# Left-over queries kept plain and scored on 64 rows per head, in an attention and maxout-FFN kernel

## The chip, the cores and the metric

The kernel runs on one core of one Trainium2 chip. The metric is the device time of one execution in microseconds. Before the change it is 326.37 us, the median of 8 runs (324.82 to 329.38).

## The reference, cut to what matters

Attention with a relative bias runs over 8 batches, 8 heads, 576 positions and 64 dimensions per head; its output, as 4608 tokens of 512, goes through a feed-forward layer with the maximum of three products.

```
scores = (q @ k.T) / 8 + bias[bucket(|i - j|)]     # per batch and head, 576 x 576
attn   = softmax(scores)                            # over the 576 keys
x      = attn @ v                                   # (8, 8, 576, 64) -> (4608, 512)
out    = max(x @ w1, x @ w2, x @ w3) @ w_out        # 512 -> 768 -> 512
```

## The kernel before

**Tiles.** 576 positions are four tiles of 128 and a rest of 64. The four tiles of keys and queries are the main part; the last 64 keys are the left-over keys, the last 64 queries the left-over queries. Two heads go together as a head pair: their 2 x 64 dimensions fill 128 partitions. For each batch b (0 to 7) and head pair hp (0 to 3) the loop of line 768 makes:

- two visits (`visit`, line 524): visit 0 scores queries 0 to 255, visit 1 queries 256 to 511, against the four key tiles. Each product runs on 64 rows, one head on partitions 0 to 63 and the other on 64 to 127, in pairs of matmuls that write different PSUM banks. ScalarE takes the exponential of each 128 x 1024 tile (`sc`).
- the left-over keys (`left_keys`, line 540): both heads at once on 128 rows. `ktail` holds the 64 keys of one head in one diagonal block and those of the other in the second, with zeros elsewhere (`diag`, line 145). They are scored for 640 query columns (512 and 128), into `el`, columns 0 to 639. The query side is kept in diagonal blocks as well (`qtail`), so the 64 left-over queries take 128 columns.
- the left-over queries (`left_queries`, line 556): four matmuls on 128 rows, each with 128 columns (64 of each head, zeros opposite), into a tile of the pool `ps_s`; one exponential writes `el` from column 640 on.
- the multiplications by exp(bias) near the diagonal, on VectorE (`times_band`, `times_bandt`, `times_band_left`).
- the products with v (`attend`, line 572), in two halves of queries, in banks of the pool `ps_a` (two buffers). A column of ones in v gives the sums; reciprocal and product (`quotients`) write `x_sb`. The half with queries 256 to 575 has two products with the left-over keys for the left-over queries (lines 594 to 598), one for each head, 65 columns each.

**Order.** The order of each engine's work is mostly written out (`inorder`). The products with v lag one head pair behind (`late`): half 0 of pair hp-1 comes after visit 0 of pair hp, half 1 after visit 1. Between visits `fill` puts groups of the FFN: each group is a `first`, `second` or `third` product of four 512-column matmuls (`ps0`, `ps1`, `ps2`), or an output block of six (`pso`), spread over the head pairs of the next batch. `fill` takes hooks, small functions that it calls before one of its groups: the last hook goes just before the last group, an earlier one before the group ahead of that. In the loop of line 768 the left-over keys are the hook of the fill after visit 0; the products with the bias for key tile 2, then the left-over queries, are the two hooks of the fill after visit 1.

**Loads.** GpSimd issues the loads of q, k and v and casts them to bf16 on the way: `load_qk` (line 162) and `load_v` (line 180). Left-over parts are loads of their own, one per parity of head (lines 160 and 170). For batches 2 to 7, SyncE then issues DMA transposes of q and k (`transposes`, line 438, issued at line 447), five steps of a q and a k transpose: steps 0 to 3 the main tiles, step 4 the left-over part of 128 rows. They are called during the batch before. In the same queue stand the transposes of the attention result (`xT<-x_sb`, line 619), issued after the quotients of the last head pair, that is in head pair 0 of the next batch, and the stores of the output (line 379). `load_v(b+1)` is called in head pair 2, 1 or 0 of batches 1, 2 and later, after visit 1 and before the fill; its target was last read by batch b-1's products with v. Batches 0 and 1 transpose on TensorE instead.

Of the kernel before, what the change touches and what calls it, by code (L numbers as in the profile page):

```python
# [39 lines left out]
def kernel(  # L40
# [12 lines left out]
    nc = tc.nc  # L53
# [64 lines left out]
    def constants(i):  # L118
        inorder(nc.vector.memset(ktail[i][:], 0.0))
        if i == 0:  # L120
            inorder(nc.vector.memset(qtail[i][:], 0.0))
        inorder(nc.vector.memset(vt[i][:], 0.0))
        inorder(nc.vector.memset(vx[i][:, :, :, D:AW], 1.0))
        for par in range(2):
            inorder(nc.vector.memset(vt[i][64 * par : 64 * par + 64, :, par, D:AW], 1.0))
# [22 lines left out]

    def q_diag(b, par, h0, h1):
        return diag(qtail[b % 2], par, h0, h1)  # L150

# [10 lines left out]
    def load_qk(b, behind=None):  # L162

        loads = []
        for t in range(KT):
            for src, dst in zip((q, k), batch[b]):
                loads.append(in_turn(b, nc.gpsimd.dma_start(out=dst[:, t], in_=main_part(src, b)[:, t])))  # L167
        for src, dst in ((q, q_diag), (k, k_diag)):
            for par in range(2):
                load = nc.gpsimd.dma_start(out=dst(b, par, 0, H), in_=tail_part(src, b, 0, H, par))  # L170
                loads.append(in_turn(b, load))
        if behind:
            for load in loads:
                tc.add_manual_dep(
                    load.ins, behind.ins.name,
                    mybir.DependencyInfo(mybir.DependencyClass.Sync, mybir.DependencyReason.DATA),
                    reason="these loads go behind the result's transposes",
                )
# [64 lines left out]
    constants(0)  # L243
    inorder(nc.vector.memset(qtail[1][:], 0.0))
    dve_copy(pick[:], ids[:])
# [15 lines left out]
    load_main(q, 0, 0, H, batch[0][0], 2, KT)  # L261
    load_tail(q, 0, 0, H, q_diag)
    load_v(0, 0, H)
# [38 lines left out]

    bandt = const.tile([P, HP, 2 * P], BF16, name="bandt")

    def make_bandt():
        for par in range(2):
            r = slice(64 * par, 64 * par + 64)
            c = BAND // 2 - 64 * par
            for c0, c1 in ((192, 256), (0, 192)):
                dve_copy(bandt[r, :, c0:c1], hank[r, par::2, c : c + c1 - c0][:, :, ::-1])  # L310

# [126 lines left out]
    def transposes(b):  # L438

        made = qk_tiles()  # L440
        qk.append(made)

        def one(j, t):
            src = batch[b][j][:, t].rearrange("p h d -> p (h d)") if t < KT else (
                (qtail, ktail)[j][b % 2][:].rearrange("p h c -> p (h c)")
            )
            inorder(nc.sync.dma_start_transpose(out=made[j][:, :, P * t : P * t + P], in_=src))

        for t in range(KT + 1):
            one(0, t)  # L450
            one(1, t)
            yield

    def qk_tiles():
        return [qkt.tile([P, HP, (KT + 1) * P], BF16, tag=n, name=n) for n in ("qT", "kT")]

# [24 lines left out]
    def more_transposes(hp):  # L481

        hs = slice(2 * hp, 2 * hp + 2)
        tp = ps_f.tile([P, 2 * CH], BF16, tag="ff", name="tp2")
        for t in range(2):
            tr(tp[:, P * t : P * t + P], batch[0][0][:, 2 + t, hs, :].rearrange("p h d -> p (h d)"), ident[:])
        tr(tp[:, QS : QS + P], qtail[0][:, hp, :], ident[:])
        dve_copy(qk[0][0][:, hp, QS:], tp[:, 0 : QS + P])

    def second_transposes(made, hp):  # L490
# [3 lines left out]
        for j, tl in enumerate((qtail, ktail)):  # L494
# [10 lines left out]
        tail = [  # L505
            copy(made[j][:, hp, KT * P :], tp[:, j, KT * P : (KT + 1) * P])
            for j, copy in enumerate((dve_copy, act_copy))
        ]
# [14 lines left out]

    def visit(qT, kT, e4, c, mid=None):


        for tt in range(0, KT, 2):
            sc = ps_s.tile([P, 2, 2, QS], F32, tag="sc", name="sc")
# [22 lines left out]
    def times_bandt(hp, el):  # L551
        inorder(nc.vector.tensor_tensor(
            out=el[:, S - 192 : S + 64], in0=el[:, S - 192 : S + 64], in1=bandt[:, hp, :], op=ALU.mult
        ))

    def left_queries(hp, qT, kT, el):

        sc = ps_s.tile([P, KT, 2 * 64], F32, tag="sc", name="scq")
        for t in range(KT):
            mm(sc[:, t, :], lhsT=kT[:, P * t : P * t + P], rhs=qT[:, QM : QM + P])  # L560
        eq = el[:, S + 64 :].rearrange("p (t h q) -> p t h q", t=KT, h=2)
        exp(eq, sc[:].rearrange("p t (h q) -> p t h q", h=2))

    def times_band_left(hp, el):
        last_tile = el[:, S + P * KT - 64 :].rearrange("p (h q) -> p h q", h=2)
        inorder(nc.vector.tensor_tensor(
# [5 lines left out]
    def attend(b, hp, e4, el, half):  # L572
# [19 lines left out]
        n = 2 + half  # L592
        if half:
            for par in range(2):
                mm(
                    x[:, 4 + par, :], lhsT=el[:, S - P + 64 * par :][:, 0:P], rhs=vl[:, hp, par, 0:AW],
                    start=True, stop=False, skip_group_check=True,
                )
                for kt in range(KT):
                    mm(  # L600
                        x[:, 4 + par, :], lhsT=el[:, S + P * kt + 64 * par :][:, 0:P],
                        rhs=v[:, kt, 2 * hp + par, 0:AW],
# [38 lines left out]
    def e_tiles():  # L641
        return (
            ep.tile([P, KT, 2, QM], BF16, tag="e4", name="e4"),
            ep.tile([P, S + 64 + KT * P], BF16, tag="el", name="el"),
        )
# [19 lines left out]
    def load_second():  # L665
        for h0, h1 in ((0, 2), (2, H)):
            load_packed(k, h0, h1, k_1)
            load_packed(q, h0, h1, q_1)
            if h0 == 0:
                load_tail(q, 1, 0, H, q_diag)  # L670
                load_tail(k, 1, 0, H, k_diag)
# [47 lines left out]
    for hp in range(HP):  # L719
# [14 lines left out]
        def keys():  # L734
            left_keys(hp, qT, kT, el, QS, S + 64)

# [31 lines left out]
    for b, hp in [(b, hp) for b in range(1, B) for hp in range(HP)]:  # L768
        if hp == 0:
            x_sb[b] = x_tile()  # L770
        qT, kT = (x[:, hp, :] for x in qk[b])
        e4, el = e_tiles()
        rate = 8 if b == 1 or (b, hp) == (2, 0) else 13

# [18 lines left out]
        if b == 1 and hp + 1 < HP:  # L793
            spread_packed(hp + 1, nc.vector)
        fill(rate, lambda: left_keys(hp, qT, kT, el, 0, S + 64))
        times_bandt(hp, el)


        visit(qT, kT, e4, 1)
        store_outputs()  # L800
# [3 lines left out]
        if turned:  # L804
            turned.pop(0)()
        quotients = next_late()
        times_band(hp, e4, 1, 0, QM, inorder)
        quotients()
        if b == 1 and hp + 1 < HP:
            second_transposes(qk[1], hp + 1)  # L810
        if hp == 1:
            add_ffn((b - 1) * CH if b > 1 else QS, CH if b > 1 else QS)
        if hp == (2, 1, 0)[min(b, 3) - 1] and b + 1 < B:
            load_v(b + 1, 0, H)
# [3 lines left out]
        if hp == 2 and 1 < b < B - 2:  # L818
            batch[b + 2] = load_tiles()
            load_qk(b + 2)  # L820

        def queries():
            left_queries(hp, qT, kT, el)
            times_band(hp, e4, 3, 0, QM, inorder)

        fill(rate, lambda: times_band(hp, e4, 2, 0, QM, inorder), queries)
        times_band_left(hp, el)
# [46 lines left out]
```

The softmax here doesn't subtract the row's maximum and nothing guards it: scores larger than these inputs give would overflow.

## Time and profile before

| what | value |
|---|---|
| time before, median of 8 runs | 326.37 us (324.82 to 329.38) |
| the profiled execution: its time, its span | 329.38 us, 327.6 us |
| TensorE matmul busy | 311.5 us, 95% of the span |
| VectorE, ScalarE, GpSimd busy | 66%, 62%, 34% |
| mean granted TensorE clock | 0.979 |
| start of visit 0, head pair 0, of batches 3 to 7 | 97.97, 133.88, 167.76, 201.64, 235.53 us |

Times within the trace count from the start of the span. A matmul row gives its latency; matmuls overlap in the pipe, so the distance between the starts of consecutive groups tells what a group occupies. The release of an engine by another is inferred from semaphore events. A DMA row of the queue SP or POOL shows the issue; the landing is later and is given apart.

### The profile page before, as it was taken

How to read it: one execution, taken by the hardware profiler on the slowest of the kernel's cores; microseconds unless marked ns; L12 is line 12 of the kernel's file. 1: busy time of each engine (PE TensorE's matmuls, PEld its weight loads, DVE VectorE, ACT ScalarE, POOL GpSimd, SP SyncE). 2: the span in 40 equal slices, each digit the busy share in tenths (PEclk: the TensorE clock that was granted, in tenths of full speed). 3: DMA queues.
4: the chain of work that ended last, by engine and by line, in shares of the span. 5: the costliest groups of instructions: out<-in, count | busy, mean ns of one | idle time of the engine just before them, and what ended most of it. 6: DMA issues, size and time to landing. Idle time of an engine off the chain costs nothing.

```text
span 327.6 us, 8019 instructions
## 1 busy us (share of the span) xinstructions
PE 311.5 (95%) x3232; PEld 177.1 (54%) x3232; DVE 216.5 (66%) x537; ACT 202.2 (62%) x274; POOL 113.0 (34%) x151
## 2 busy tenths in 40 slices
PE   7847999999997999999999999999999999999995
PEld 2335776787554555555555555555555554444442
DVE  6466788778665766776667777676667675554452
ACT  4837798788676667776776677757776661121221
POOL 8931967209756772096107810500000000000000
PEclk9869899999999999999999999999999999999999
DMA  9999999979999999999999999995132103301103
GB/s 166 171 207 198 152 156 132 147 141 118 159 166 155 161 159 191 133 109 168 209 96 102 180 208 78 97 186 145 13 66 83 55 3 67 136 0 64 66 0 128
DMA packets 165541, 40.72 MB, mean 124 GB/s; under 512 B 155384, under 2 KB 161024, under 8 KB 165504
## 3 DMA queue, kind: packets, MB, share of 16 engines
q0 software_dynamic: 103904, 16.66, 77.0%
q1 hardware_dynamic: 59840, 23.08, 38.1%
q10 hardware_dynamic: 1760, 0.47, 0.7%
q8 instruction: 25, 0.41, 0.5%
q14 instruction: 12, 0.10, 0.1%
HBM read 35.39 MB, written 9.45 MB: 137 GB/s over the span
## 4 chain that ended last, share of the span: by engine, by line
PE 82%; DMA 6%; ACT 3%; POOL 3%; DVE 3%; issue 1%; SPq 0%; POOLq 0%; ACTq 0%
PE ps L94 40%; PE a L94 15%; PE pso L94 13%; PE sc L94 9%; DMA kT<-k_sb 3%; PE sct L94 3%; DMA vt<-in_v_dram 2%; ACT e L522 2%; PE scq L94 2%; POOL q_sb L143 1%; POOL vx L143 1%; DVE e L516 1%; PE tp L97 1%; DMA out_dram<-osb 1%; ACT el L522 1%
## 5 line engine op out<-in xcount | busy, mean ns | idle before, releaser
L94 PE MATMUL ps<-xT,w_bf 128*128 128x512 bf16 (+1 forms) x720 | 156.6, 359 | 0.0
L522 ACT ACTIVATE e<-sc 128x1024 bf16<-128x1024 f32 x128 | 124.5, 1025 | 26.7 <-PE sc L94 26.1
L94 PEld LDWEIGHTS <-w_bf 128*128 128x128 bf16 x720 | 66.1, 98 | 57.1 <-issue 1.5
L516 DVE TENSOR_TENSOR e<-e,hank 128x512 bf16<-128x512 bf16 (+2 forms) x136 | 59.7, 467 | 27.3 <-ACT e L522 24.8
L337 ACT ACTIVATE m<-ps 128x512 bf16<-128x512 f32 x54 | 32.3, 599 | 66.8 <-PE ps L94 64.5
L343 DVE TENSOR_TENSOR m<-ps,m 128x512 bf16<-128x512 f32 x54 | 37.3, 691 | 45.9 <-ACT el L522 24.5
L94 PEld LDWEIGHTS <-kT 64*128 64x128 bf16 (+1 forms) x704 | 35.8, 96 | 41.2 <-issue 23.7
L94 PE MATMUL pso<-wo_bf,hT 128*128 128x512 bf16 (+2 forms) x222 | 51.0, 373 | 0.0
L94 PE MATMUL a<-vx,e 128*128 128x65 bf16 x1024 | 46.0, 195 | 0.0
L94 PE MATMUL sc<-qT,kT 64*128 64x256 bf16 x512 | 41.6, 276 | 3.8 <-DMA kT<-k_sb 1.7
L143 POOL DMA_DIRECT2D vx<-in_v_dram x32 | 28.5, 900 | 44.7 <-PE a L94 39.7
L94 PE MATMUL a<-vt,el 128*128 128x130 bf16 (+1 forms) x192 | 40.0, 215 | 4.0 <-DMA vt<-in_v_dram 4.0
L94 PEld LDWEIGHTS <-e 128*128 128x128 bf16 x1024 | 41.7, 99 | 1.0 <-issue 0.2
L348 DVE TENSOR_TENSOR hT<-ps,m 128x512 bf16<-128x512 f32 x54 | 37.1, 686 | 5.1 <-PE ps L94 3.3
L609 DVE TENSOR_TENSOR x_sb<-a,rd 128x256 bf16<-128x256 f32 (+1 forms) x64 | 31.4, 491 | 2.2
L94 PEld LDWEIGHTS <-el 128*128 128x128 bf16 x448 | 24.3, 97 | 15.3 <-issue 10.2
L110 DVE COPY osb<-pso 128x512 f32<-128x512 f32 (+1 forms) x33 | 22.7, 688 | 13.5 <-PE pso L94 10.0
L94 PEld LDWEIGHTS <-hT 128*128 128x128 bf16 x222 | 20.2, 97 | 20.6 <-DVE hT L348 0.4
L167 POOL DMA_DIRECT2D q_sb<-in_q_dram x24 | 22.1, 921 | 18.5 <-DVE x_sb L609 14.8
L522 ACT ACTIVATE el<-sct 128x640 bf16<-128x640 f32 (+2 forms) x36 | 23.2, 646 | 5.7 <-PE sct L94 5.2
L167 POOL DMA_DIRECT2D k_sb<-in_k_dram x24 | 21.9, 914 | 6.1 <-DMA vx<-in_v_dram 3.2
L522 ACT ACTIVATE el<-scq 128x512 bf16<-128x512 f32 x32 | 19.0, 595 | 6.6 <-PE scq L94 6.6
(69 smaller groups left out, 170.8 us busy)
## 6 DMA issues: line engine op xcount, KB each, us to landing
out_dram<-osb SPq DMA_DIRECT2D x35, 256.0 KB, 2.9
vx<-in_v_dram POOLq DMA_DIRECT2D x32, 128.0 KB, 6.2
q_sb<-in_q_dram POOLq DMA_DIRECT2D x26, 128.0 KB, 9.2
k_sb<-in_k_dram POOLq DMA_DIRECT2D x24, 128.0 KB, 9.3
w_bf<-in_moe_w_dram POOLq DMA_DIRECT2D x3, 768.0 KB, 14.0
xT<-in_k_dram SPq DMA_DIRECT2D x6, 128.0 KB, 4.4
hank<-w_dr SPq DMA_DIRECT2D x2, 384.0 KB, 7.7
wo_bf<-in_moe_w_out_dram POOLq DMA_DIRECT2D x1, 768.0 KB, 9.4
```

What stands on the lines that cost most here:

```text
L94: inorder(nc.tensor.matmul(*args, **kw))
L97: inorder(nc.tensor.transpose(*args))
L110: return inorder(nc.vector.tensor_copy(out_, in_))
L143: in_turn(b, nc.gpsimd.dma_start(out=dst[:, t, h0:h1, :], in_=x[:, t, h0:h1, :]))
L167: loads.append(in_turn(b, nc.gpsimd.dma_start(out=dst[:, t], in_=main_part(src, b)[:, t])))
L337: nc.scalar.activation(out=st[fb]["m0"][:], in_=ps0, func=ACTF.Copy)
L343: inorder(nc.vector.tensor_tensor(out=m[:], in0=ps1, in1=st[fb]["m0"][:], op=ALU.max))
L348: inorder(nc.vector.tensor_tensor(out=hT[:, fb * CH : fb * CH + CH], in0=ps2, in1=st[fb]["m"][:], op=ALU.max))
L516: put(nc.vector.tensor_tensor(out=e4[:, t, :, lo:hi], in0=e4[:, t, :, lo:hi], in1=hank[:, 2 * hp : 2 * hp + 2, c0:c1][:, :, ::-1], op=ALU. ...
L522: nc.scalar.activation(out=out_, in_=in_, func=ACTF.Exp, scale=inv_sqrt_d)
L609: divided[b, hp, half] = inorder(nc.vector.tensor_tensor(out=x_sb[b][:, 2 * half : 2 * half + n, P * hp : P * hp + P].rearrange("p t (h d) ...
```

## The change

- `qtail` keeps the left-over queries plain: 64 rows (queries) by 2 x 64 dimensions, no diagonal blocks. One load per batch (`load_q_tail`) takes the place of two. The rows 64 to 127 are zeroed once. The DMA transposes of the left-over queries take 64 rows, and `qT` has 576 columns for 640.
- The left-over queries are scored on 64 rows per head: eight matmuls of 64 columns, in pairs, for four of 128 columns on 128 rows.
- In the head pairs with `together` (all but those of batches 0 and 1 and the first of batch 2: 23 of 32) these matmuls and two exponentials stand at the start of visit 1, in two banks of the pool `ps_a`. In the other nine they stay in the fill, with one exponential.
- With `together`, the products with v after visit 1 (`attention`) move into the first hook of the fill, so that they come behind one FFN group.
- The left-over keys are scored for 576 columns for 640; the product with the bias beside them covers 192 columns for 256; the two 65-column products with v of the left-over keys become one of 130.
- The fill after visit 1 stands ahead of `load_v` and `load_qk` in program order.

```diff
+    def load_q_tail(b):
+        dst = qtail[b % 2][0 : S - KT * P].rearrange("p g (h d) -> p (g h) d", h=2)
+        return in_turn(b, nc.gpsimd.dma_start(out=dst, in_=q[b, :, KT * P : S, :].rearrange("h p d -> p h d")))
...
-        for src, dst in ((q, q_diag), (k, k_diag)):
-            for par in range(2):
-                load = nc.gpsimd.dma_start(out=dst(b, par, 0, H), in_=tail_part(src, b, 0, H, par))
-                loads.append(in_turn(b, load))
+        loads.append(load_q_tail(b))
+        for par in range(2):
+            load = nc.gpsimd.dma_start(out=k_diag(b, par, 0, H), in_=tail_part(k, b, 0, H, par))
+            loads.append(in_turn(b, load))
...
+            n = P if t < KT or j else S - KT * P
...
-            inorder(nc.sync.dma_start_transpose(out=made[j][:, :, P * t : P * t + P], in_=src))
+            inorder(nc.sync.dma_start_transpose(out=made[j][:, :, P * t : P * t + n], in_=src))
...
+    def put_left_queries(el, banks):
+
+        eq = el[:, S:].rearrange("p (t h q) -> p t h q", t=KT, h=2)
+        for par, bank in enumerate(banks):
+            exp(eq[:, :, par, :], bank.rearrange("p (t q) -> p t q", t=KT))
+
+    def turn_left_queries(qT, kT, banks):
+
+        for t in range(KT):
+            for par, bank in enumerate(banks):
+                r = slice(64 * par, 64 * par + 64)
+                mm(bank[:, 64 * t : 64 * t + 64], lhsT=kT[r, P * t : P * t + P], rhs=qT[r, QM:S])
+
+    def visit(qT, kT, e4, c, mid=None, el=None):
+
+        if el is not None:
+            banks = [ps_a.tile([P, KT * 64], F32, tag="a", name="scq") for _ in range(2)]
+            turn_left_queries(qT, kT, banks)
+            put_left_queries(el, banks)
...
     def left_queries(hp, qT, kT, el):
 
-        sc = ps_s.tile([P, KT, 2 * 64], F32, tag="sc", name="scq")
-        for t in range(KT):
-            mm(sc[:, t, :], lhsT=kT[:, P * t : P * t + P], rhs=qT[:, QM : QM + P])
...
+        sc = ps_s.tile([P, 2, CH], F32, tag="sc", name="scq")
+        turn_left_queries(qT, kT, [sc[:, par, 0 : KT * 64] for par in range(2)])
...
+            mm(
+                x[:, 4:6, :], lhsT=el[:, S - P : S], rhs=vl[:, hp, :, 0:AW],
+                start=True, stop=False, skip_group_check=True,
+            )
             for par in range(2):
-                mm(
-                    x[:, 4 + par, :], lhsT=el[:, S - P + 64 * par :][:, 0:P], rhs=vl[:, hp, par, 0:AW],
-                    start=True, stop=False, skip_group_check=True,
-                )
...
+        together = b > 1 and (b, hp) != (2, 0)
...
-        fill(rate, lambda: left_keys(hp, qT, kT, el, 0, S + 64))
+        fill(rate, lambda: left_keys(hp, qT, kT, el, 0, S))
...
-        visit(qT, kT, e4, 1)
+        visit(qT, kT, e4, 1, el=el if together else None)
...
-        quotients = next_late()
-        times_band(hp, e4, 1, 0, QM, inorder)
-        quotients()
+        def attention():
+            quotients = next_late()
+            times_band(hp, e4, 1, 0, QM, inorder)
+            quotients()
+
+        if not together:
+            attention()
...
+        def queries():
+            if not together:
+                left_queries(hp, qT, kT, el)
+            times_band(hp, e4, 3, 0, QM, inorder)
+
+        def keys_2():
+            if together:
+                attention()
+            times_band(hp, e4, 2, 0, QM, inorder)
+
+        fill(rate, keys_2, queries)
         if hp == (2, 1, 0)[min(b, 3) - 1] and b + 1 < B:
             load_v(b + 1, 0, H)
...
-        def queries():
-            left_queries(hp, qT, kT, el)
-            times_band(hp, e4, 3, 0, QM, inorder)
-
-        fill(rate, lambda: times_band(hp, e4, 2, 0, QM, inorder), queries)
```

## The prediction, made before the changed kernel was run

> **What bounds the kernel now.** I read the page first, then the windows by batch, then the timeline of one head pair, and last the waits and the landings of the DMA transposes. The page:
>
> ```profile
> PE 311.5 (95%) x3232; PEld 177.1 (54%) x3232; DVE 216.5 (66%) x537; ACT 202.2 (62%) x274; POOL 113.0 (34%) x151
> ...
> PEclk9869899999999999999999999999999999999999
> DMA  9999999979999999999999999995132103301103
> ```
>
> TensorE is busy nearly all the time, at full clock after the first few slices; the DMA engines are saturated until about slice 27. The windows of batches 3 (rest), 4 and 5:
>
> ```profile
> 104.00:131.80 27.80, 27.80 (x317) 15.68 (x317) 19.46 (x47) 19.42 (x25) 15.63 (x21) 1.00 1.84 169
> 131.80:165.70 33.90, 33.90 (x369) 18.77 (x368) 23.70 (x57) 23.66 (x31) 14.64 (x19) 1.00 1.72 152
> 165.70:199.60 33.90, 33.90 (x370) 18.76 (x369) 23.71 (x57) 23.66 (x31) 14.29 (x18) 1.00 1.53 150
> ```
>
> Columns: stretch, its us, busy us of PE, PEld, DVE, ACT, POOL, granted clock, DMA share. PE is busy for all of each stretch; DVE and ACT have 30% free. So a column taken from TensorE is time gained, unless a wait takes its place. What a group occupies is seen from start to start in the timeline (PE, batch 5):
>
> ```profile
> 187.58 0.43 PE L94 MATMUL sct<-qT,kT 128*128 128x512 bf16 x2
> 187.85 1.03 PE L94 MATMUL ps<-xT,w_bf 128*128 128x512 bf16 x4
> 188.81 0.61 PE L94 MATMUL sc<-qT,kT 64*128 64x256 bf16 x8
> 189.35 0.23 PE L94 MATMUL a<-vt,el 128*128 128x130 bf16 x1
> ...
> 190.26 1.89 PE L94 MATMUL ps<-xT,w_bf 128*128 128x512 bf16 x8
> 191.99 0.39 PE L94 MATMUL scq<-qT,kT 128*128 128x128 bf16 x4
> 192.21 1.03 PE L94 MATMUL ps<-xT,w_bf 128*128 128x512 bf16 x4
> ```
>
> Eight 512-column matmuls take 191.99 - 190.26 = 1.73 us, 216 ns each, or 0.42 ns a column. The left-over queries take 0.22 us, the left-over keys 0.27. From 187.85 to 188.81 four matmuls should take 0.86 and take 0.96: about 0.10 us is lost on going from 128 rows to 64. The eight on 64 rows take 0.54; four pairs of 256 columns are 4 x 0.107 = 0.43, so again 0.10 goes on the way back.
>
> **The change, part by part: TensorE.**
>
> *Left-over queries on 64 rows.* They now take 4 pairs of 64 columns. Does a pair run at once? A window of the first 0.1 us of that visit:
>
> ```profile
> 188.81 0.28 PE L94 MATMUL sc<-qT,kT 64*128 64x256 bf16 x2
> ```
>
> Two have begun within 0.1 us and their union is 0.28, the latency of one: yes. Then a pair costs 64 x 0.42 = 27 ns, four 0.11 us. No row has 64-row pairs that short; the upper bounds are the nearest row, 65-column matmuls with a weight load each (eight in 189.66 - 189.42 = 0.24, 30 ns), if both of a pair count, 8 x 30 = 0.24; and worse, see the second rival. I take 0.135, near the low end, because the 64-row visit runs at its column rate apart from the two switches. The Trainium skill ("TensorE: Matmul & The Clock Gate", section "Wait — 56ns, not 53.3ns?") says that starts never come closer than about 25 ns however few the columns. By it eight matmuls cost 0.20, a gain of 0.02; by the row (two starts within one latency) 0.135, a gain of 0.08. I go by the row, since the rule's figure is for a plain row of matmuls.
>
> *The switch.* With `together` the eight stand directly before the 64-row visit, so the 0.10 + 0.10 are paid once as now. In the other nine pairs they stand between 128-row groups: +0.20.
>
> *Left-over keys* lose 64 columns: -0.027. *The 130-column product* for two of 65: 0.06 to 0.057, -0.005.
>
> Sum per pair: with `together` -0.08 - 0.027 - 0.005 = -0.113 us; otherwise -0.113 + 0.20 = +0.08.
>
> **ScalarE and the banks.** Two exponentials for one in the 23 pairs:
>
> ```profile
> L522 ACT ACTIVATE el<-scq 128x512 bf16<-128x512 f32 x32 | 19.0, 595 | 6.6 <-PE scq L94 6.6
> ...
> L522 ACT ACTIVATE el<-sct 128x256 bf16<-128x256 f32 x4 | 1.5, 407 | 0.0
> ```
>
> These are rows of the groups with shapes apart; the fields are busy us, mean ns of one, idle before. 2 x 0.41 for 0.60 is +0.22 us, and the visit's own exponentials come 0.8 us later: with visit 1 at T, scores of the left-over queries at T+0.14, their exponentials until T+1.15, the two large ones (1.94 together) until T+3.1. Who waits? The products with v take the first of the two banks only after one FFN group, at T + 0.67 + 0.86 = T+1.5, while its exponential ends near T+0.75: covered by 0.75. VectorE's products with the bias for key tile 2 then end about T+4.1; the next pair's half 0 needs them at T+4.8: covered by 0.7. Without that cover each late 0.1 us would cost 23 x 0.1. I cost both at nothing. VectorE's shorter product (64 of 256 columns fewer) and the shorter `sct` exponential lie off the path: nothing.
>
> **Loads and transposes.** One issue less per batch on GpSimd (0.65 us of two) moves later issues forward; at the start (chain: `qtail` loads, then `vx`, `vt`, then PE waits 4.0 us) the DMA engines are saturated with the same bytes, so I take nothing, between 0 and -0.6. The 64-row transpose halves one of ten. PE now waits 1.7 and 0.4 us in batch 3:
>
> ```profile
> 100.14 0.28 PE L94 MATMUL sc<-qT,kT 64*128 64x256 bf16 x2 [1.67 <-DMA kT<-k_sb]
> ...
> 102.86 0.11 PEld L94 LDWEIGHTS <-kT 128*128 128x128 bf16 x2 [0.51 <-DMA kT<-ktail]
> ```
>
> The second is behind the left-over queries' transpose, so I take -0.2 of its 0.4 (between 0 and -0.4). The first isn't touched, and it swallows what batch 2's three `together` pairs gain (3 x 0.113).
>
> **Where a new wait may come.** With `attention` behind an FFN group, half 1 of the last pair (in head pair 0 of the next batch) comes about 0.9 us later, and on it hang two queues: SyncE's transposes of the result with all key and query transposes behind them, and GpSimd's `load_v`, `load_qk` behind it. In a window of batch 4, ahead of that point and after:
>
> ```profile
> 140.70:141.50 0.80, 0.80 (x8) 0.52 (x7) 0.80 (x3) 0.14 (x1) 0.80 (x2) 1.00 0.05 3
> 141.50:168.00 26.50, 26.50 (x287) 14.49 (x286) 18.51 (x45) 18.44 (x24) 12.60 (x17) 1.00 1.91 166
> ```
>
> The DMA engines stand idle, then are saturated for 26.5 us: if both queues start 0.9 late, the landings come up to 0.9 late. The last key tile for batch 5, from the answer on its transpose:
>
> ```profile
> L447 SPq DMA_TRANSPOSE kT<-k_sb x1: 1786/1786/1786, 158.2 to 158.2; - x1
> ...
> DMA to landing us min/median/max: 8.9/8.9/8.9
> ```
>
> It lands at 167.1; PE's visit starts at 167.76 and needs it for its fourth pair, 0.33 later: 1.0 us to spare. For batch 6, the same answer gives 191.2 + 9.9 = 201.1 against 201.64 + 0.33: 0.9 to spare. The change takes 0.9 by the delay and 4 x 0.113 = 0.45 by TensorE's gain in between: short by 0.3 to 0.45, so a wait of about 0.35 us at batches 5 and 6, and I take the same for batch 4, whose landing isn't shown (it did arrive by 134.2). From batch 7 on no loads follow and the transposes come with time to spare.
>
> **Sum**, against the profiled execution (span 327.6, its own time 329.38): nine pairs x 0.08 = +0.7, of which waits that PE has anyway in batches 0 and 1 hide over half: +0.3; batch 2 nothing; batch 3's second wait -0.2; 20 pairs of batches 3 to 7 x -0.113 = -2.26; new waits 3 x 0.35 = +1.05. Together -1.1, 328.3. It is the slowest of eight runs, 3.0 above the median; the terms are the same in any run, so from 326.37: 325.2.
>
> **Rivals.**
>
> 1. *The transposes still land in time* (the saturated engines make up the delay: landing is 8 us behind issue). Then no new wait, -0.2 - 2.26 + 0.3 and perhaps a few tenths at batch 3: 324.0. For: SyncE's issue isn't what bounds the landing. Against: the engines are idle just before, so lost time isn't made up. Chance 0.30.
>
> 2. *Slower: the short matmuls don't cover their weight loads.* Place: the eight at the head of visit 1. A weight load row on 64 rows reads 93 ns; in the visit, 107 ns of columns cover it, here 27. The skill (same page, "The mechanism") says that a weight load overlaps a running matmul only when the row groups differ; by that a pair would cost about 27 + 93 = 0.12, four 0.48, +0.23 a pair after the keys: 20 x 0.23 + half of 9 x 0.43 = 6.5, so 332.9. Against it: 65-column matmuls on the same rows go at 30 ns, so loads do overlap there. It decides from 62 ns a pair on (0.22 + 0.03 = 4 x 62). At 95 ns a pair, the load alone, +0.13 each and +0.33 in the nine: 20 x 0.13 + half of 9 x 0.33 = 4.1, and no new wait comes: 330.5. Chance 0.12.
>
> 3. *The pairs run one after the other*, 0.24: -0.01 a pair, +0.18 for the nine, half hidden, new waits about 0: 327.0. The saving isn't had, which is the case of a change that doesn't do what it says. Chance 0.12.
>
> **How the numbers follow.** Main case 0.46 at 325.2 (own range 324.2 to 327.5, as the new waits are 0.1 to 0.8 each and the nine pairs +0.1 to +0.7). What measurement can tell from no change is about 0.5%, 1.6 us: faster is below 324.7, slower above 328.0. Faster: all but a little of rival 1 (0.27) and a third of the main case (0.15): 0.42. Slower: rival 2, and 0.05 of the others: 0.17. Same: 0.41. Range 323.3 to 328.2: it leaves out most of rival 2 and a little below rival 1.
>
> **What would show it.** Right: in the 23 pairs `scq` to `sc` in about 0.14 us on 64 rows; batches 3 to 7 each 0.45 us shorter where no wait stands; a wait of `sc` on the DMA of `kT` of some 0.3 us at the starts of batches 4 to 6; in batches 0 and 1 0.1 us of lost time on each side of `scq`. Wrong: `scq` at 0.24 or more, PE waiting for ACT or DVE at `a`, or waits on `kT` beyond 1 us.

## The result, and the profile after

The change makes the kernel slower. The changed kernel takes 333.14 us, the median of 11 runs (327.9 to 340.7), where the kernel before took 326.31 in the same session (32 runs, 324.39 to 330.22). The ratio is 1.0124, interval 1.0085 to 1.0163. The ratios of this text leave out executions more than 1.5% above a kernel's fastest; as six of the changed kernel's eleven are, its median, 2.1% longer, lies further from 1 than its ratio. Forecast were 325.2 us and a range of 323.3 to 328.2.

The profiled execution of the changed kernel, at 327.9 us (span 326.1), is the quickest of its runs, while the one shown of before (329.38) was the slowest of its first eight. So the two traces are compared by their stages, not by their ends. First the page of the changed kernel:

```profile
PE 306.7 (94%) x3328; PEld 171.3 (53%) x3328; DVE 213.1 (65%) x535; ACT 201.6 (62%) x297; POOL 108.2 (33%) x143
...
PEclk9979999999999999999999999999999999999999
DMA  9999999959999999999989999699123103301103
...
PE 55%; DMA 19%; issue 7%; POOL 6%; SPq 6%; ACT 3%; DVE 2%; POOLq 0%; ACTq 0%
```

TensorE is busy for 4.8 us less (306.7 for 311.5), but not all of this is the change: 3.0 us of it lie before the start of batch 1, where the execution shown of before had more of half clock (PEclk; 0.979 as the mean of the whole, for 0.995). And the chain that ended last now runs through DMAs for 19% of the span. In the kernel before that line of the page read:

```profile
PE 82%; DMA 6%; ACT 3%; POOL 3%; DVE 3%; issue 1%; SPq 0%; POOLq 0%; ACTq 0%
```

So the DMA work has become part of what sets the end. What TensorE waited for between 60 and 235 us (columns: total us, times, longest), before and then after:

```profile
PE sc L94 <- DMA kT<-k_sb: 1.7, 1, 1.7
```

```profile
PE sc L94 <- DMA kT<-k_sb: 5.0, 5, 1.7
PE sct L94 <- DMA kT<-ktail: 0.8, 2, 0.5
```

One wait for the main keys (`k_sb`) has become five, one at the start of each batch from 2 to 6. The timeline shows them at the last pair of the first visit, which needs the last key tile (bracket: idle before, and the releaser), here for batches 2 to 6 in turn:

```profile
66.00 0.28 PE L94 MATMUL sc<-qT,kT 64*128 64x256 bf16 x2 [0.87 <-DMA kT<-k_sb]
...
97.75 0.28 PE L94 MATMUL sc<-qT,kT 64*128 64x256 bf16 x2 [1.72 <-DMA kT<-k_sb]
...
132.55 0.28 PE L94 MATMUL sc<-qT,kT 64*128 64x256 bf16 x2 [0.63 <-DMA kT<-k_sb]
...
166.93 0.28 PE L94 MATMUL sc<-qT,kT 64*128 64x256 bf16 x2 [0.67 <-DMA kT<-k_sb]
...
201.59 0.28 PE L94 MATMUL sc<-qT,kT 64*128 64x256 bf16 x2 [1.15 <-DMA kT<-k_sb]
```

The starts of visit 0, head pair 0, by the traces (us):

| batch | 1 | 2 | 3 | 4 | 5 | 6 | 7 | 7 to end |
|---|---|---|---|---|---|---|---|---|
| before | 39.7 | 68.2 | 98.0 | 133.9 | 167.8 | 201.6 | 235.5 | 92.1 |
| after | 35.9 | 64.6 | 95.5 | 131.4 | 165.8 | 199.9 | 234.6 | 91.5 |
| after, a second execution (330.66) | 35.0 | 63.7 | 98.8 | 133.9 | 168.6 | 202.8 | 237.4 | 91.5 |

The changed kernel starts batch 2 some 3.6 us earlier than before, and by batch 7 has 0.9 of that left. In the second execution, batch 2 takes 35.1 us for 29.8 before (a wait and half clock, below), and batches 4 to 6 together 1.8 us more. Where nothing waits, as from batch 7 on, the changed kernel is 0.6 us quicker.

### The profile page after: what moved, and what is told of

Read it like the earlier page. It is cut to its first block, busy times and chain, and to the rows that moved or that the text cites. A ratio compares the mean times of both kernels' runs of the same rounds, so it can differ in the third digit from the quotient of the medians.

```text
span 326.1 us, 8238 instructions
## 1 busy us (share of the span) xinstructions
PE 306.7 (94%) x3328; PEld 171.3 (53%) x3328; DVE 213.1 (65%) x535; ACT 201.6 (62%) x297; POOL 108.2 (33%) x143
## 4 chain that ended last, share of the span: by engine, by line
PE 55%; DMA 19%; issue 7%; POOL 6%; SPq 6%; ACT 3%; DVE 2%; POOLq 0%; ACTq 0%
PE ps L94 28%; PE pso L94 10%; PE a L94 9%; DMA kT<-k_sb 6%; SPq L448 6%; DMA k_sb<-in_k_dram 5%; PE sc L94 5%; DMA kT<-ktail 5%; DMA vt<-in_v_dram 2%; ACT e L523 2%; POOL vx L143 2%; PE sct L94 1%; POOL q_sb L168 1%; PE scq L94 1%; POOL q_sb L143 1%
## 5 line engine op out<-in xcount | busy, mean ns | idle before, releaser
L94 PEld LDWEIGHTS <-w_bf 128*128 128x128 bf16 x720 | 64.1, 98 | 60.7 <-issue 5.0
L94 PEld LDWEIGHTS <-kT 64*128 64x128 bf16 (+1 forms) x832 | 29.6, 95 | 42.5 <-issue 24.6
L94 PE MATMUL a<-vt,el 128*128 128x130 bf16 x160 | 35.8, 224 | 3.7 <-DMA vt<-in_v_dram 3.7
L523 ACT ACTIVATE el<-scq 128x256 bf16<-128x256 f32 (+1 forms) x55 | 20.5, 416 | 10.9 <-PE scq L94 10.7
L523 ACT ACTIVATE el<-sct 128x576 bf16<-128x576 f32 (+2 forms) x36 | 21.6, 605 | 5.8 <-PE sct L94 5.4
```

Of the source, the lines that this page charges most:

```text
L94: inorder(nc.tensor.matmul(*args, **kw))
L523: nc.scalar.activation(out=out_, in_=in_, func=ACTF.Exp, scale=inv_sqrt_d)
```

## The experiments

All runs together. Each ratio is to the kernel before, run on the same chip in the same session.

| run | median us (n) | ratio, 95% interval |
|---|---|---|
| e1 changed, attention directly in head pair 0 | 333.71 (6) | 1.0223 [1.0172, 1.0274] |
| e2 before, attention later in head pair 0 | 326.7 (12) | 1.0057 [1.0027, 1.0087] |
| e3 changed, transposes earlier | 327.35 (10) | 1.0051 [1.0019, 1.0083] |
| e4 changed, transposes of 128 rows | 332.87 (6) | 1.0239 [1.0196, 1.0282] |
| e5 before, with the change's transfers | 327.41 (22) | 1.0022 [0.9996, 1.0049] |
| e6 before, with the change's order and rows | 330.62 (6) | 1.0146 [1.0102, 1.0191] |
| e7 changed, two loads of left-over queries | 329.92 (6) | 1.0144 [1.0101, 1.0188] |
| e8 changed, value loads of batch 2 later | 328.78 (12) | 1.0082 [1.0052, 1.0112] |
| e9 changed, head pair 0 as before | 330.67 (6) | 1.0135 [1.0087, 1.0184] |
| e10 changed, edits of e3 and e8 | 326.68 (22) | 0.9988 [0.9958, 1.0017] |
| e11 before, edits of e3 and e8 | 327.62 (22) | 1.0026 [1.0005, 1.0047] |
| e12 as e10, key loads of batch 3 earlier | 323.76 (12) | 0.9929 [0.9893, 0.9965] |
| e13 before, all three edits | 326.93 (22) | 1.0034 [1.0012, 1.0057] |
| e14 changed, all edits but that of e3 | 327.45 (18) | 1.0059 [1.0030, 1.0089] |
| e16 as e10, matmuls in batch 3's wait | 325.47 (22) | 0.9995 [0.9968, 1.0022] |
| e17 the changed kernel again | 330.66 (1) | one execution |

**Which part costs: transfers, order, or transpose shape.** e4 gives the left-over queries' transposes their 128 rows back (`n = P`). e5 puts the change's plain queries, its single load and its transposes into the kernel before; e6 puts in only the new order and the 64-row matmuls, on the old diagonal blocks; e7 splits the single load in two. e5 leaves out the separation of the two heads in the left-over scores: its products have the old sizes and places, on columns that don't fit them.

```diff
-        return in_turn(b, nc.gpsimd.dma_start(out=dst, in_=q[b, :, KT * P : S, :].rearrange("h p d -> p h d")))
+        return [
+            in_turn(b, nc.gpsimd.dma_start(
+                out=dst[:, h0 : h0 + 4], in_=q[b, h0 : h0 + 4, KT * P : S, :].rearrange("h p d -> p h d")))
+            for h0 in (0, 4)
+        ]
```

> The changed kernel, but the left-over queries are transposed over all 128 rows (64 of them zero) as before. Theory A: no difference from the changed kernel, 332 to 334. Theory B (64-row transposes hold up the queue): goes down to about 326.

> The kernel before with the data movement of the change alone: the left-over queries loaded plain in one load, transposed over 64 rows, qT of 576 columns; TensorE's products keep the number, the size and the place that they had before (their last 128 query columns are columns 448 to 575, so the left-over queries and keys are scored with the wrong columns and both heads mixed). Theory D (the plain load and the shorter chain on GpSimd move the loads of batches 0 to 2 against the DMA transposes, which land late for batch 2 and then for each batch): slow, 331 to 334. Theory E (the 64-row products, their place and the delayed products with v cost the time): 325 to 326, as before.

> The other part alone: diagonal blocks, two loads, 128-row transposes and 640 columns as before, but the left-over queries scored on 64 rows per head from those blocks, at the head of visit 1 in the banks of the AV sums with two exponentials, the products with v behind an FFN group, and the fill ahead of load_v. Theory D: 325 to 326. Theory E: 331 to 334.

> The changed kernel with the plain left-over queries in two loads of four heads each for the single one. Theory D in its narrow form (the single load itself, by its size or its place in GpSimd's queue): 325 to 327. Otherwise 331 to 334.

e4 stays at 332.87, so the transpose's shape isn't the cause. For the transfers alone (e5) the interval includes no difference; but 8 of its 22 runs lie above 328.0 us, the highest of the kernel before in that session, and its trace, of a run of 331.25 us, has waits of 5.2 us at batch 2. So the ratio doesn't show all that they do. The order with the short matmuls costs 1.5% (e6); in its trace TensorE waits 0.85, 0.57 and 1.32 us at batches 4 to 6, there for the left-over keys (`ktail`). The single load does one thing: batch 1 begins at 34.6 to 35.9 us in the twelve traces that have it, at 36.7 to 39.7 in the six with two loads (37.2 in e7, which differs from the changed kernel in this alone). It didn't shorten the kernel: with two loads e7 is as slow by its ratio, and by its median 1.3% longer than before, where the changed kernel is 2.1%; six runs don't tell whether that is a difference.

**The delay of the transposes.** e1 takes the delay out of the changed kernel by doing `attention` directly behind visit 1 in head pair 0 (`if not together or hp == 0`); e2 puts the delay alone into the kernel before; e9 gives head pair 0 its old order whole; e3 leaves the delay but begins the transposes one head pair earlier from batch 3 on:

```diff
-        elif hp and b + 1 < B:
-            if hp == 1:
+        elif (hp or b > 2) and b + 1 < B:
+            if hp == (1 if b == 2 else 0):
                 crossbar = transposes(b + 1)
-            next(crossbar)
+            next(crossbar, None)
...
-        if b == 1 or hp in (1, 2) and b + 1 < B:
+        if b == 1 or (hp in (1, 2) or hp == 0 and b > 2) and b + 1 < B:
```

> The changed kernel, but in head pair 0 of batches 3 to 7 the products with v and their quotients stand directly behind visit 1 again, as before the change; the other head pairs keep them behind an FFN group. Theory A (the transposes of the result, and the loads of v, q and k behind them, start 0.9 us later in head pair 0, and the key transposes for the next batch then land after its first visit): the waits of sc on the DMA of kT at the starts of batches 4 to 7 go back to about 0.3 us or none; TensorE pays some 0.2 us five times for the bank; time about 324.5, and a narrow spread. Theory B (the single load and the 64-row transposes of the left-over queries cost the time): stays near 331 to 333. Theory C (the two exponentials and the two banks hold TensorE up): stays near 331 to 333, with waits on ACT at the products with v.

> The kernel before, with one thing of the change alone: in head pair 0 of batches 3 to 7 the products with v after visit 1 stand behind one FFN group (and load_v behind the fill). Theory A: the landing of the last key transposes shifts by 0.9 us, which takes up the 0.9 to 1.0 us to spare in the profile of before; waits of 0 to 0.5 us at the starts of batches 4 to 6 in a quick run and more in others: 327 to 330, and a wider spread than before. Theories B and C: 326.3, the same as before.

> The changed kernel, but from batch 3 on the DMA transposes for the next batch begin in head pair 0 and not in head pair 1, so that their first steps stand ahead of the transposes of the result in SyncE's queue. Theory A: the last key transpose lands some 3 us ahead of the visit that needs it, no waits at batches 4 to 7; 323.5. Theory B and C: near 331 to 333.

> The changed kernel, but head pair 0 of every batch is done as before the change in order (attention directly behind visit 1, left-over queries in the fill, on 64 rows); the other three head pairs keep the new order. So SyncE's transposes and GpSimd's loads start as before, and only 0.4 us per batch of TensorE's gain is left. Theory G (the keys' transposes of the next batch set each batch's start since they begin later and TensorE comes earlier): the waits at batches 4 to 6 shrink from 0.7 to 1.2 us to 0 to 0.5 us each, batch period near 33.9, time about 327 (325 to 330), the rest above the kernel before being waits at batches 2 and 3. Rival (the later start does not matter, transfers are simply slower with plain queries): waits at batches 4 to 6 stay near 1 us, time near 333.

e1 failed as a test: without the FFN group, the products with v began 0.1 us late in each head pair 0 (by the distances between starts, 0.64 for 0.54), as it seems for the banks that the left-over queries held, and what follows them another 0.2; the waits for keys at batches 4 to 6 didn't go, and its trace is of its longest execution. e2 has the delay in a kernel whose TensorE is not faster (and, like the change, the fill ahead of the loads): +0.57%, about 1.9 us, with batches 4 to 6 0.1 to 0.3 us longer each (34.08, 34.15, 33.97 for 33.89). These make 0.5 us; where the rest of the 1.9 lies, its trace, of one of its shorter runs, doesn't show. In e3 all waits from batch 4 on are gone and the ratio falls from 1.0124 to 1.0051. e9 removes the delay cleanly. Its batch 5 in the timeline:

```profile
167.59 0.38 PE L94 MATMUL ps<-xT,w_bf 128*128 128x512 bf16 x1
167.91 0.61 PE L94 MATMUL sc<-qT,kT 64*128 64x256 bf16 x8
```

The visit's eight matmuls run through without a bracket: the last keys had landed at 166.99, 1.25 us before they were needed, and 1.18 at batch 6. That is as the theory has it, but the time stays at 330.67, since its trace has waits at batches 2, 3 and 4 (1.5, 3.4 and, for the left-over keys, 1.6 us). So the delay makes the waits at batches 5 and 6; it is not the whole loss.

**Batches 2 and 3.** e8 holds the value loads of batch 2 back, so that they no longer share the DMA engines with batch 2's keys:

```diff
...
-            load_v(b + 1, 0, H)
+            load_v(b + 1, 0, H, divided[1, 1, 1] if b == 1 else None)
```

(the last argument makes the loads wait for a product of batch 1). e10 is e8 and e3 together, e11 the same two edits on the kernel before. e12 adds a third, on the query and key loads of batch 3:

```diff
-            load_qk(3, divided[1, HP - 1, 1])
+            load_qk(3, divided[1, HP - 2, 1])
```

e13 is the kernel before with all three, e14 the changed kernel with all but that of e3.

> The changed kernel with the loads of v for batch 2 held until the quotients of batch 1, head pair 1, half 1 are done (about 4 us later). Theory F (these loads compete with the transposes for batch 2, so that its first visit waits 1 to 5 us, TensorE's clock drops, and batch 3's loads start later too): the wait at the start of batch 2 falls to below 1 us and the time to 327 to 329. Otherwise 331 to 334.

> The changed kernel with two edits to the order of its transfers: the value loads of batch 2 are held behind the last transposes of batch 1's queries and keys having been used (so they no longer share the DMA engines with batch 2's keys), and from batch 3 on the transposes for the next batch begin in head pair 0 in place of 1. Theory G: no wait on keys at batch 2 of over 1 us and none from batch 4 on, period 33.35, wait at batch 3 of 1.5 to 3.5 us stays; time about 324.3 (323 to 326). Rival (the paired matmuls cost TensorE itself more than the profile shows): 328 or more, with no wait on keys in the chain.

> The kernel before with the same two edits to the order of its transfers. Theory G: it had no wait on keys but the one at batch 3, so it gains little: 326.0 (325 to 327). The difference to the changed kernel with the same edits is the worth of the change to TensorE with the transfers off its path: 5 batches at about 0.54 us, some 2 us in favour of the changed one. Rival (the edits to the order of transfers are a gain by themselves): it gains as much as the changed kernel does, and the difference is 0.

> As the changed kernel with both edits, and the query and key loads of batch 3 are let go one head pair of batch 1 earlier (some 7 us). Theory G: batch 3's first wait (1.7 us before the change) goes too, so some 1.5 us more than with the two edits alone: 322.8 (322 to 325). Rival (the earlier loads collide with batch 2's transposes, which then land later): the wait moves to batch 2, time as with the two edits or 1 to 3 us longer.

> The kernel before with all three edits to the order of its transfers (value loads of batch 2 held back, transposes from batch 3 on begun a head pair earlier, query and key loads of batch 3 let go a head pair earlier). Theory G: it is TensorE's shorter work that pays in the changed kernel with these edits (323.8), so the kernel before with them stays 2 us or more behind it: 326 (325 to 327). Rival (the gain of that version comes from the order of the transfers alone): 324 or less, no difference between the two.

> The changed kernel with the two edits that concern batches 2 and 3 alone; from batch 3 on the transposes start where the change put them. Theory G: the waits at batches 2 and 3 are gone, those of 0.4 to 1.2 us at batches 4 to 6 stay, so 1.5 to 3 us above the version with all three edits: 326 (325 to 327.5). If the start of the transposes in batches 3 to 5 is the whole loss: 330 or more. If it is no part of it: 324.

e8 recovers a part, 328.78: batch 2 waits only 1.2 us, for its left-over keys, but batch 3 then waits 3.6. e10 missed: 326.68 for the 324.3 expected. Batch 2 still waits 1.5 us, for its left-over keys, batch 3's wait is at the upper end of what was expected, and something comes after it. Its timeline and windows there (behind the busy times of the five engines stands the granted clock):

```profile
98.82 0.40 PE L94 MATMUL sc<-qT,kT 64*128 64x256 bf16 x2 [3.49 <-DMA kT<-k_sb]
```

```profile
90.00:94.00 4.00, 3.95 (x54) 2.32 (x54) 2.51 (x6) 3.20 (x6) 2.10 (x3) 1.00 1.53 190
94.00:98.00 4.00, 1.33 (x11) 0.41 (x8) 2.22 (x6) 1.62 (x2) 1.75 (x2) 0.93 2.16 147
98.00:102.00 4.00, 3.18 (x25) 1.86 (x26) 0.61 (x2) 1.02 (x1) 2.90 (x4) 0.50 1.81 133
102.00:106.00 4.00, 3.87 (x27) 1.63 (x27) 1.37 (x3) 1.67 (x4) 1.65 (x3) 0.72 2.47 164
```

After 3.5 us of waiting TensorE ran at half clock until about 104 us. Batch 3 took 39.57 us there, 36.1 less its wait; the quick execution of the changed kernel took 35.89, less its waits of 1.72 and 0.49 us 33.7. So the half clock cost about 2.4 us on top of the wait.

e12 shortens that wait to 0.8 us (and another 0.7 before the left-over keys, which land at 99.2) and lies within its expected range: 323.76, faster than before by 0.7%. Its batches 4, 5 and 6, and then those of e13:

```profile
129.74:163.08 33.34, 32.81 (x375) 18.15 (x381) 23.35 (x57) 23.58 (x34) 13.72 (x17) 1.00 1.72 152
163.08:196.42 33.34, 32.81 (x375) 18.16 (x382) 23.35 (x57) 23.58 (x34) 13.73 (x17) 1.00 1.52 141
196.42:229.76 33.34, 32.81 (x375) 18.16 (x381) 23.34 (x57) 23.57 (x34) 4.77 (x6) 1.00 0.81 102
```

```profile
132.25:166.14 33.89, 33.89 (x371) 18.78 (x370) 23.68 (x56) 23.64 (x31) 14.29 (x18) 1.00 1.58 150
166.14:200.01 33.87, 33.87 (x369) 18.75 (x368) 23.68 (x56) 23.63 (x31) 14.29 (x18) 1.00 1.46 141
200.01:233.90 33.89, 33.89 (x369) 18.79 (x369) 23.68 (x56) 23.64 (x31) 4.78 (x6) 1.00 0.81 106
```

With the transfers off the path, a batch of the changed kernel is 0.54 us shorter (33.34 for 33.88), every time. (The first rows are six matmuls short of the changed kernel's 381, so their busy time is too low.) The kernel before gains nothing from the same edits (e11, e13: 1.003), which give it a new wait for the transposed attention result, in e13:

```profile
PE ps L94 <- DMA xT<-x_sb: 1.6, 1, 1.6
```

So it is the change that pays in e12, by 1.0034 - 0.9929, about 1% or 3.4 us, once the transfers allow it. But TensorE's shorter work is only a part of that. The two traces lie 4.7 us apart (span 321.3 for 326.0): batches 4 to 6 give 1.6 of it and batch 7 to the end 0.6, while e12 is 2.7 us ahead already at the start of batch 1 (35.3 for 38.0), as the traces with the single load are. In the changed kernel itself the waits at batches 2 to 6 use that lead up.

e14 tells the parts of the loss apart, though in its trace batch 2 still waits 1.3 us and batch 3 0.6 and 0.9, waits that were expected to be gone. Without the earlier transposes 1.0059, with them 0.9929: the starts of batches 4 to 6 are worth 1.3%. Without the edits to batches 2 and 3 (e3) 1.0051, with them 0.9929: 1.2%. Neither alone explains the loss.

**The half clock.** e16 puts 24 pairs of matmuls that are overwritten afterwards into e10's wait at batch 3; e17 is a second execution of the changed kernel with its profile.

```diff
...
+                for i in range(extra if tt + t == KT - 1 else 0):
+                    for par in range(2):
+                        r = slice(64 * par, 64 * par + 64)
+                        mm(sc[:, par, t, :], lhsT=kT[r, 0:P], rhs=qT[r, c * QS : c * QS + QS])
...
```

> The changed kernel with the two edits of the experiment that took the chain off the path (value loads of batch 2 held back, transposes from batch 3 on begun earlier), and 48 extra matmuls of 256 columns on 64 rows per head (24 pairs x 0.107 = 2.6 us; their scores are overwritten, the result is the same) in the first visit of batch 3, directly before the pair that waits 3.5 us for its keys. They only fill the wait. Theory C (a wait of over some 3.5 us is followed by half clock, which costs 2.5 us on top): the wait left is about 1 us, no window of batch 3 below clock 0.9, and the batch from 3 to 4 takes 36.9 us where it took 39.6; median 325 (324 to 326.5) for 326.7, and few runs above 328. Rival (half clock has another cause, or doesn't cost): the time stays at 326.7 or rises by up to 2.6 us.

> The changed kernel itself, for the profile of another execution, since the one shown first was the quickest of eleven. Theory G with C: the batches less their waits take 29.6 (batch 2) and 33.4 us (3 to 6), and what is above that is half clock after waits of 3.5 us or more at batches 2 or 3; in an execution of about 333 us the waits add up to 8 to 11 us instead of 6.3. Rival: the longer time is spread over batches without waits or half clock.

e16's median is within the noise of e10's (0.9995 and 0.9988). In its trace the keys landed at 96.3, so the wait covered would have been 1.8 us, not 3.5, and the extra work cost 0.8; the clock was 1.00 from 92 to 112 us, but a wait of 1.8 us was in no trace followed by half clock, so this trace doesn't test Theory C. One of its 22 runs lies above 329 us, five of e10's 22. That fits with it, but doesn't decide what half clock costs on average.

e17 (330.66 us) shows it at batch 2, in the windows and the timeline:

```profile
60.00:64.00 4.00, 4.00 (x67) 3.04 (x65) 3.36 (x8) 3.41 (x6) 0.00 (x0) 1.00 1.47 128
64.00:68.00 4.00, 0.18 (x4) 0.00 (x0) 1.04 (x4) 1.35 (x2) 0.00 (x0) 1.00 1.50 116
68.00:72.00 4.00, 3.90 (x33) 2.84 (x34) 1.30 (x3) 1.35 (x2) 0.00 (x0) 0.57 0.46 149
72.00:76.00 4.00, 4.00 (x67) 2.91 (x65) 2.68 (x7) 3.20 (x5) 0.31 (x1) 1.00 0.21 41
```

```profile
68.10 0.28 PE L94 MATMUL sc<-qT,kT 64*128 64x256 bf16 x2 [3.92 <-DMA kT<-k_sb]
```

TensorE idles for 3.9 us, then has 33 matmuls in a window that holds 67 before and after. Less its wait, batch 2 takes 31.2 us where the quick execution, less its waits of 0.87 and 0.31, has 29.7: 1.5 us for the half clock. Its waits for keys sum to 8.1 us between 60 and 235 us, those of the quick one to 5.8. With batch 2 begun 0.9 earlier, 2.3 + 1.5 - 0.9 = 2.9 comes to about the 2.8 us between the two executions.

## Why the prediction was wrong

**TensorE's gain: right in mechanism, a little too small.** The left-over queries in batch 5 of the changed kernel:

```profile
169.94 0.81 PE L94 MATMUL ps<-xT,w_bf 128*128 128x512 bf16 x3
170.69 0.29 PE L94 MATMUL scq<-qT,kT 64*128 64x64 bf16 x8
170.81 0.60 PE L94 MATMUL sc<-qT,kT 64*128 64x256 bf16 x8
```

Eight starts fill 170.81 - 170.69 = 0.12 us; 0.135 was forecast, and the 25 ns a start that the prediction set beside it would have made 0.20. The measurement decides: it is 15 ns a start. Pairs do run at once, and their weight loads are covered: rivals 2 and 3 are out. The sum per batch was 0.45; where nothing waits (e3, e10, e12) it is 0.54. In the changed kernel itself, less what the last pair of the first visit is late (its start, less that of the visit, less the 0.33 it takes without a wait), it is 0.35, 0.54 and 0.54 at batches 4 to 6. What makes the 0.09 above the forecast isn't shown.

**The nine other pairs**: 0.08 us each was forecast. Batch 1 takes 28.70 for 28.49, 0.05 for each of its four.

**ScalarE and the banks at nothing**: right. Between 60 and 235 us the changed kernel's TensorE waits for nothing but keys. e1 shows that the cover was needed: with the FFN group gone from in front of it, `attention` came 0.1 us late.

**Early loads at nothing: this step failed.** I argued that saturated DMA engines carry the same bytes as before. But with one load in place of two batch 1 begins some 3 us earlier (35.9 and 35.0 for 39.7 in the traces of the kernels themselves), while batch 2's last keys land at 66.0, in the second execution at 68.1, for 67.7. So TensorE comes to batch 2 before its keys, which I hadn't considered: 0.87 us in the quick execution, 3.9 in the second. There this term, with the 1.5 us of half clock behind it, costs 5.4 us, more than the earlier start had gained.

**Batch 3**: the first wait was to stay as it was and did, 1.72 for 1.67 us, and in the quick execution it swallowed batch 2's gain as forecast. The second was to shrink by 0.2 and didn't: TensorE stands idle there for 0.49 us, where before the bracket, of 0.51, stood at a weight load alone. In e8, e9 and e10 the first is 3.4 to 3.6 us.

**The new waits: the main step that failed, in its size.** Place and cause were right. Visit 1 of head pair 0 of batch 4 and the first load for the next batch, before and then after:

```profile
137.99 0.61 PE L94 MATMUL sc<-qT,kT 64*128 64x256 bf16 x8
...
139.81 0.90 POOL L143 DMA_DIRECT2D vx<-in_v_dram  x1 [7.66 <-PE a L94]
```

```profile
136.62 0.60 PE L94 MATMUL sc<-qT,kT 64*128 64x256 bf16 x8
...
139.30 0.90 POOL L143 DMA_DIRECT2D vx<-in_v_dram  x1 [17.87 <-PE a L94]
```

The load comes 2.68 us behind the visit, where it came 1.82 behind: 0.86 more, 0.9 was forecast. The term was 3 x 0.35 = 1.05. Measured are 0.63, 0.67 and 1.15, together 2.45, in the quickest execution. It was mis-sized at the landing. The answer on batch 5's last key tile in the changed kernel:

```profile
L448 SPq DMA_TRANSPOSE kT<-k_sb x1: 2654/2654/2654, 157.3 to 157.3; - x1
...
DMA to landing us min/median/max: 9.6/9.6/9.6
```

It is issued earlier than before (157.3 for 158.2), as the whole batch is, yet lands at 166.9 for 167.1. From visit 1 of head pair 0 of the batch before, the last keys for batches 5 and 6 land after 30.3 and 30.7 us, where they took 29.1 and 29.2: 1.1 and 1.5 us more, not 0.86. TensorE needs them 0.63 earlier, not 0.45 (29.47 for 30.10 after that visit). So the loop from one batch's visit 1 through the transfers to the next batch's keys is 0.8 and 1.3 us longer than TensorE's own work, and it repeats at each batch. In e2, with the delay and the order of the loads alone, the shift is 0.9 to 1.1. What makes up the rest in the changed kernel isn't settled.

**What the sum left out.** I carried the terms from one trace to the median with "the same in any run". That held only while TensorE set the end. Once it arrives before the keys at every batch, each late landing counts in full, and a long one can be followed by half clock: the runs spread over 13 us for 6 before. e12, where the transfers are put in time, comes near rival 1 (in time, 324.0), but in part by luck: it has the earlier start of batch 1, which no sum of the prediction had. The slower ending was there under a falsifier, "waits on `kT` beyond 1 us", and not as a rival with a price.

**The clock gate.** The Trainium skill ("TensorE: Matmul & The Clock Gate", section "Part 1: The HAM clock gate") says that about one idle window of 3.4 us halves the clock, and that the window runs free of the kernel. The traces agree with the second, and with the length: within a trace, the clock changes at distances that are multiples of 3.41 us, and the grid that this makes lies differently in each. With the first they agree in part. Half clock followed a wait of 3.49 us in e10 but not one of 3.43 in e9, and it followed one of 2.18 in e3 but not one of 2.18 in e14. Cut along the grid, the traces tell why, first e3, then e9 (the second figure behind the stretch is TensorE's busy time):

```profile
63.43:66.84 3.41, 1.23 (x22) 0.78 (x21) 1.45 (x5) 2.03 (x4) 0.00 (x0) 1.00 1.42 173
66.84:70.26 3.42, 3.42 (x26) 2.41 (x23) 1.30 (x3) 1.36 (x2) 0.00 (x0) 0.50 0.35 95
```

```profile
94.17:97.58 3.41, 1.65 (x12) 0.57 (x10) 2.53 (x6) 1.62 (x2) 1.56 (x2) 1.00 1.85 157
97.58:100.99 3.41, 1.75 (x25) 1.15 (x26) 0.61 (x2) 1.02 (x1) 1.22 (x3) 1.00 2.03 107
100.99:104.40 3.41, 3.41 (x45) 1.94 (x44) 1.55 (x3) 2.11 (x4) 3.41 (x5) 1.00 2.39 166
```

In e3 the wait lies in one window, which is idle for 2.18 us; in e9, with the grid carried on from the changes at the start of the trace, a border halves it, 1.76 and 1.66. So it is in all traces of this case, between 40 and 300 us: the eight windows at full clock with 2.10 to 3.21 us idle (e1 twice, e3, e4, e5, e8, e10, e17) were each followed by half clock, and no other, the idlest 1.76. A window needn't be wholly idle, then, and what decides is where the wait falls on the grid.

How much of the 333 us is half clock stays open in part, as only two executions of the changed kernel have a profile. But the mean granted clock of each of the eleven is on record: 0.990 to 1.000 in the five up to 332.2 us, 0.969 to 0.985 in the six from 333.1 us. The lost clock times the span comes to 5.1 us more in the six, which are 6.2 us longer on average. By this estimate half clock is up to 5.1 of the 6.2; it is less where it falls into a wait, and no run tests it. The ratio of 1.0124 rests on the five, so half clock has little part in it.

## What to carry to other kernels

Before speeding up the engine that bounds a kernel, follow the loop that feeds it (here keys land, are scored, the attention result frees the queues, the next keys are transferred) and compare its slack with the gain plus every delay that the change puts into it; about 1 us of slack against 0.45 of gain and 0.9 of delay means that the feed takes over. From then on the spread of the transfers is the spread of the kernel, and long waits can cost clock as well. Then the same change may still pay, once the transfers are started earlier: here a ratio of 1.0124 became 0.9929, with three edits that gain nothing in the kernel before.

## What was not expected of the hardware

- Eight matmuls of 64 columns on alternate halves of the rows, each with its own weight load, filled 0.12 us, 15 ns a start.
- Half clock in mid-kernel came after each window of 3.41 us in which TensorE was idle for 2.10 us or more, and after none with 1.76 or less. Beyond the wait it cost about 1.5 us (e3, e17), 2.4 (e10) and, after 5.2 us of waits, 3.1 (e5).
- One load of eight heads for two of four each, with the same bytes, went with a start of batch 1 at 34.6 to 35.9 us for 36.7 to 39.7, the DMA engines being saturated. Why is not shown.
